# Turning the activations from a second copy in memory instead of on TensorE, in a fused attention and gated-MLP kernel

## The chip, the cores and the metric

The kernel runs on one core of one Trainium2 chip. The metric is the device time of one execution in microseconds. Three runs of the kernel before gave 1763.13 to 1763.9 us, with a median of 1763.62 us. Engines are called as in the profile: PE is TensorE, DVE VectorE, ACT ScalarE, POOL GpSimd, SP the engine whose queue starts most DMAs.

## What is computed

The input x is 2048 rows of 512. Each row is normalised (mean taken away, divided by its standard deviation), and the normalised rows xn go into two branches that are multiplied at the end:

```python
xn = _layernorm(x, axis=-1)
s = _A_ref(xn, A_k_cache, A_v_cache, A_wq, A_wo)      # attention, 32 heads of 128, last 512 keys
g = _silu(_B_ref(xn, B_w_in, B_w_sp, B_b_sp, B_w_out)) # gated MLP
return x + s * g

# in _A_ref
q = (x @ wq).reshape(B, Sq, Hq, Dh)                    # then per head:
scores = einsum("bhqd,bhkd->bhqk", q, k) * Dh ** -0.5
o = einsum("bhqk,bhkd->bhqd", softmax(scores), v);  out = o @ wo
# in _B_ref
z = _gelu(x @ w_in); z1, z2 = z[..., :Fh], _layernorm(z[..., Fh:])
out = (z1 * (einsum("ts,bsf->btf", w_sp, z2) + b_sp[None, :, None])) @ w_out
```

All of it is float32. [...]

## The kernel before

A product `x @ w` needs x with its 512 columns on the partitions. x comes from memory with rows on the partitions, so each tile of 128 rows is normalised and then turned by four TensorE transposes against an identity matrix into one PSUM bank (`flip`, L215). From there ACT casts the high part and DVE or POOL subtracts it from the whole (`rest`, L59), which gives the low part.

The 16 row tiles are two halves of eight. The queries are made by a seven-product scheme over 2 x 2 blocks (`q_products`, L473): besides blocks of x itself it needs four sums of blocks, called T1 to T4, as high and low parts. They are built from tile p and tile 4 + p of a half, p from 0 to 3.

The program is one list written by hand. After a prologue that normalises and turns tiles 0 to 3 (`ln_open`, `ln_apply`, `ln_flip`) comes a loop over steps t from -7 to 529. In each step every engine's queue gets its work in a fixed order: a turn of one early tile, the split of the probabilities of an earlier block (`shares`, t - 11), whatever the tables `todo`, `ends` and `loads` hold for this step, one score tile of 128 x 512 (`score`), products of the next queries, probabilities times values (`pv`, t - 13), the output projection (`outp`, t - 18), and the 32 x 32 transposes of the step before (`turn`). Each engine takes its list in order, and so does SP's DMA queue: a wait holds up all that stands behind it.

Two places of it matter here.

- **The opening's second turn.** In steps -3 to 0 `t_sums(p)` turns tile p once more and `row_sums` (L250 to L252, DVE) makes three sums of its PSUM bank and of the turned tile 4 + p, which stands in `sacc`. In the step after, `t_split(p)` casts four quarters on ACT (L263) and subtracts four times on POOL. Score 0 stands in step 0 behind `t_sums(3)`. A score is read by DVE (`nm`, L500, the row maximum), then by ACT (`prob`, L502, the exponential). Scores, outputs and early pieces of the MLP product take turns on the four PSUM buffers called ps_3 (`ps_step`). In steps -2 to 2 these are, the second turns left away, in order: a piece, a piece, score 0, a piece, score 1, a piece, score 2; score 2 comes into the buffer of score 0. The exponential frees a score's buffer.
- **The second half's x.** `later_x(p)` handles tiles 8 + p and 12 + p, in a list of steps that begins at t = 30 and goes on every 2.6 steps until t = 214. It loads both tiles as rows (pool `xq`, tiles called rawx, five buffers), takes the statistics on DVE (L177), scales the tile on ACT (L315), turns it on TensorE into a ps_a bank (L215), and from that bank makes copies (ACT), low parts and sums (DVE, deferred to the end of the step by the list `late`). All parts go to memory and come back when the second half starts.

POOL's share of a steady step is the low part of the probabilities (`pT_l<-pL,pT_h`, L59), which `pv` needs two steps later (L540), and beside it the low parts of weights (`wl<-raw,wh`, `x<-wq`) and sums of weights (L442). Statistics go through `ln_scale`, which ends in a power on POOL (L75).

Of the kernel before, what the change touches and what calls it, by code (L numbers as in the profile page):

```python
# [17 lines left out]
P = 128  # L18
S, D = 2048, 512
H, DH, W = 32, 128, 512  # L20
NT = S // P
NC = D // P
# [12 lines left out]
T8 = NT // 2  # L35
# [2 lines left out]


@with_exitstack  # L40
def mixer_kernel(ctx: ExitStack, tc: tile.TileContext, x, wh, w_in, w_sp, b_sp, w_out, out):

# [7 lines left out]
    nc = tc.nc  # L50
# [3 lines left out]
    dram = ctx.enter_context(tc.tile_pool(name="dram", bufs=1, space=DRAM))  # L54
# [3 lines left out]
    def rest(engine, lo, whole, hi):  # L58
        engine.tensor_tensor(lo, whole, hi.bitcast(F32), op=OP.subtract)  # L59

    late = []
# [10 lines left out]
    def rsqrt(var, y, n, v, engine=nc.gpsimd):  # L72

        engine.tensor_scalar(v[:, :n], var, EPS, None, op0=OP.add)
        nc.gpsimd.tensor_tensor(y[:, :n], v[:, :n], power[:, :n], op=OP.pow)  # L75

    stats = ctx.enter_context(tc.tile_pool(name="stats", bufs=2))
# [9 lines left out]
    ap = att.enter_context(tc.tile_pool(name="ap", bufs=2))  # L87
# [74 lines left out]
    def halves(t):  # L162
        return t.rearrange("p (c q) -> p c q", q=P)
# [9 lines left out]
    def tile_stats(t, key, k):  # L173
        if k == 0:
            mv[key] = stats.tile([P, 2, 2], F32, name="mv", bufs=5)
        stt = stats.tile([P, 6], F32, name="stt", bufs=4)
        nc.vector.bn_stats(stt, t)  # L177
        nc.vector.bn_aggr(mv[key][:, k, :], stt)
# [4 lines left out]
        ln_scale(len(tiles), key)  # L183

    def ln_scale(n, key):
        r = stats.tile([P, 2], F32, name="rs_r", bufs=5)
        tmp[key] = stats.tile([P, 2], F32, name="rs_t", bufs=4)
        rsqrt(mv[key][:, :n, 1], r, n, tmp[key], nc.vector)
        for k in range(n):
            rx[key + k] = mv[key][:, k, 0:1], r[:, k:k + 1]  # L190

    def ln_open(i):
        a, b = next(g for g in GROUPS if g[0] <= i < g[1])
# [18 lines left out]
    def flip(t, late=False):  # L212
        ps = ps_acc.tile([P, NC, P], F32, name="ps_a") if late else ps_step.tile([P, NC, P], F32, name="ps_3")
        for c in range(NC):
            nc.tensor.transpose(ps[:, c, :], t[:, c * P:(c + 1) * P], ident)  # L215
        return ps
# [31 lines left out]
    def row_sums(ps, y, o):  # L248

        nc.vector.tensor_tensor(o[:, :256], y[:, :256], ps[:, :256], op=OP.subtract)  # L250
        nc.vector.tensor_tensor(o[:, 256:], ps[:, :256], y[:, 256:], op=OP.add)
        nc.vector.tensor_tensor(y[:, :256], ps[:, 256:], o[:, 256:], op=OP.subtract)  # L252

    def t_sums(p):
# [41 lines left out]

    def later_x(p):

        a, b = T8 + p, T8 + 4 + p
        t, nb = {}, {}  # L300
# [6 lines left out]
        def row_stats():  # L307
            ln_scale(2, 100 * (p + 1))
            for k, i in enumerate((a, b)):
                mean, r = rx[100 * (p + 1) + k]  # L310
                nb[i] = tmp[100 * (p + 1)][:, k:k + 1]
                nc.gpsimd.tensor_scalar(nb[i], mean, r, -1.0, op0=OP.mult, op1=OP.mult)

        def apply(i):
            nc.scalar.activation(t[i], t[i], AF.Identity, bias=nb[i], scale=rx[100 * (p + 1) + (i == b)][1])  # L315

        def parts(i, n):
            ps = flip(t[i], True).rearrange("p c q -> p (c q)")
            x = t["x", n] = xq.tile([P, 512], F32, name="rawx")
            nc.scalar.copy(x, ps)  # L320
            if n:
                st = t[0, 1] = xq.tile([P, 512], F32R, name="rawx")
                nc.scalar.copy(st[:, :256], ps[:, :256])
                late.append((rest, nc.vector, st[:, 256:], ps[:, :256], st[:, :256]))
                late.append((rest_f32, t[b][:, 256:], ps[:, 256:], x[:, :256]))
            else:
                late.append((sums, ps, t["x", 1], t[b], t[a]))

        def rest_f32(to, x0, x1):
            nc.vector.tensor_tensor(to, x0, x1, op=OP.subtract)  # L330

        def sums(ps, x, y, o):
            nc.vector.tensor_tensor(o[:, :256], x[:, :256], ps[:, :256], op=OP.subtract)
            nc.vector.tensor_tensor(o[:, 256:], ps[:, :256], y[:, 256:], op=OP.add)
            nc.vector.tensor_tensor(y[:, :256], ps[:, 256:], o[:, 256:], op=OP.subtract)

        def store(*ks):
            for k in ks:
                if k in WHOLE:
                    src, h = {"T1": (a, 0), "T2": (a, 1), "T4": (b, 0), "T3": (b, 1)}.get(k) or (("x", k[1]), k[0])  # L340
                    nc.sync.dma_start(xd[1, k][:, :, p * P:(p + 1) * P], halves(t[src][:, 256 * h:256 * h + 256]))
                else:
                    nc.sync.dma_start(xd[1, k][:, :, :, p * P:(p + 1) * P],
                                      t[k].bitcast(F32).rearrange("p (a c q) -> p a c q", a=2, q=P))

        seq = [load, None, None, lambda: tile_stats(t[a], 100 * (p + 1), 0), lambda: tile_stats(t[b], 100 * (p + 1), 1),
               row_stats, None,
               lambda: apply(b),
               lambda: parts(b, 1),
               lambda: apply(a),  # L350
               None,
               lambda: parts(a, 0)] + [None] * 5
        stores = {10: ((0, 1), (1, 1)), 13: ((0, 0), (1, 0)), 14: ("T2",), 15: ("T1",), 16: ("T3",), 17: ("T4",)}
        return [(f, stores.get(n, ())) for n, f in enumerate(seq + [None])], store


# [209 lines left out]

    T0, T1 = -QL, NSTEP + OL
    NG = NBLK // 4
    todo, mid = {}, {}

    def at(t, f, *args):
        todo.setdefault(t, []).append((f, args))
# [70 lines left out]
    for p in range(4):  # L643
        seq, store = later_x(p)
        for k, (f, ks) in enumerate(seq):
            t = max(t + 2, 30 + 13 * n // 5)
            while k in (8, 11) and t % 4 != 2:
                t += 1
            for key in ks:
                at(t, store, key)  # L650
            if f:
                (mid if k in (8, 11) else todo).setdefault(t, []).append((f, ()))
            n += 1

    load_x(0, 1)
# [72 lines left out]
    for t in range(T0, T1):  # L728
        if t % 4:
            load_all(t)  # L730
        bq, cq = divmod(t + QL, 4)
        bm, cm = divmod(t - ML, 4)
        bp, cp = divmod(t - PL, 4)
        bo, jo = divmod(t - OL, 4)
        i = t + XL
        if i < T8:
            ln_flip(i)
        if 0 <= bm < NBLK:
            shares(bm, cm)
        for f, args in todo.get(t, ()):  # L740
            f(*args)
        if 0 <= t < NSTEP:
            score(t)
        if i + 2 < T8:
            ln_apply(rows[i + 2], i + 2)
        if t in FILL:
            z1_piece(*FILL[t])
        if 0 <= bq < 4:
            qproj(bq, cq)
        g, s = divmod(t + LEAD, 16)  # L750
        if 0 < g < NG:
            q_products(g, s)
        for f, args in mid.get(t, ()):
            f(*args)
# [12 lines left out]
        if t in DRAIN:  # L767
            z1_out(*DRAIN[t], ps)
        if 0 <= t - 1 < NSTEP:
            turn(t - 1)  # L770
        if t % 4 == 2 and 0 <= t // 4 - 1 < NBLK:
            turned(t // 4 - 1)
        while late:
            f, *args = late.pop(0)
            f(*args)
        if t % 4 == 0:
            load_all(t)
        for f, *args in ends.get(t, ()):
            f(*args)
# [425 lines left out]
```

## Time and profile before

| | |
|---|---|
| three runs, median | 1763.62 us |
| profiled execution, its own time | 1763.41 us |
| its span in the profile | 1761.6 us |
| PE busy | 1754.7 us |
| DVE / ACT / POOL busy | 1491.0 / 1186.7 / 1226.6 us |
| granted TensorE clock, mean | 1.0 |
| DMA | 394.25 MB, 224 GB/s |

The span runs from the first to the last instruction that the profile shows; the profiled execution's own time has 1.8 us more, around the span. Busy time adds an engine's instructions up. A row of the timeline has the start in microseconds from the span's start, the duration, the engine, the line of the kernel, the operation and what it writes and reads; `x4` merges four that follow each other; a bracket tells how long the engine sat idle before it and what ended that.

### The profile page before, as it was taken

What the parts mean: (1) busy time and instruction counts of PE and PEld (TensorE: products, weight loads), DVE (VectorE), ACT (ScalarE), POOL (GpSimd) and SP (SyncE); (2) the same over time, 40 slices, a digit from 0 to 9 for tenths busy, and PEclk for the clock granted to TensorE, in tenths of its full rate; (3) what the DMA queues carried; (4) which work ended last, traced back from release to release, by engine and by line L of the source; (5) the groups of instructions that cost most, each with busy time, mean ns of one, the idle gap of its engine ahead of it and who ended that gap; (6) DMA issues with size and microseconds to landing.
All of it is one profiled execution on the core that took longest, in us unless ns stands there. A gap on an engine that the chain in (4) does not pass through costs nothing.

```text
span 1761.6 us, 28515 instructions
## 1 busy us (share of the span) xinstructions
PE 1754.7 (100%) x8463; PEld 1506.7 (86%) x8463; DVE 1491.0 (85%) x2470; ACT 1186.7 (67%) x2621; POOL 1226.6 (70%) x1151
## 2 busy tenths in 40 slices
PE   9999999999999999999999999999999999999999
PEld 8888888888888888888888888888888899999997
DVE  6789989898998989988888888888888647887875
ACT  5777777777777777777777777777777546543333
POOL 2889888888888889878888888888888411000032
PEclk9999999999999999999999999999999999999999
DMA  5688887888888889787887877877788652655496
GB/s 203 209 236 253 247 248 233 248 240 236 251 241 239 250 231 272 217 262 223 224 224 221 229 227 220 226 222 219 232 226 247 216 194 86 224 187 177 148 257 206
DMA packets 171708, 394.25 MB, mean 224 GB/s; under 512 B 23840, under 2 KB 53792, under 8 KB 152352
## 3 DMA queue, kind: packets, MB, share of 16 engines
q1 hardware_dynamic: 166944, 386.80, 74.8%
q10 hardware_dynamic: 4608, 5.64, 0.9%
q8 instruction: 66, 1.08, 0.3%
q14 instruction: 90, 0.74, 0.1%
HBM read 229.55 MB, written 162.79 MB: 223 GB/s over the span
## 4 chain that ended last, share of the span: by engine, by line
PE 98%; DMA 1%; DVE 0%; ACT 0%; issue 0%; SPq 0%; ACTq 0%
PE ps_a L473 17%; PE ps L65 13%; PE ps L67 13%; PE ps L66 13%; PE ps L906 11%; PE ps_a L540 6%; PE ps_a L539 6%; PE ps_a L538 6%; PE ps_a L67 2%; PE ps_a L66 2%; PE ps_a L65 2%; PE ps_f L67 1%; PE ps_f L66 1%; PE ps_f L65 1%; PE ps_f L906 1%; DMA pL<-p_dram 1%
## 5 line engine op out<-in xcount | busy, mean ns | idle before, releaser
L59 POOL TENSOR_TENSOR pT_l<-pL,pT_h 128x512 fp32r<-128x512 f32 x507 | 658.0, 1301 | 185.1 <-ACT pT_h L530 176.1
L502 ACT ACTIVATE prob<-ps,nm 128x512 f32<-128x512 f32 x512 | 354.0, 691 | 339.7 <-DVE nm L500 331.6
L562 DVE SCALAR_TENSOR_TENSOR sacc<-ps,sums,sacc 128x512 f32<-128x512 f32 x496 | 369.8, 746 | 119.2 <-PE ps L67 114.0
L473 PE MATMUL ps_a<-x,x 128*128 128x512 f32 x1266 | 365.3, 389 | 0.0
L511 DVE STREAM_TRANSPOSE pL<-prob 128x512 f32<-128x512 f32 x512 | 358.8, 701 | 0.5 <-ACT prob L502 0.4
L500 DVE TENSOR_REDUCE nm<-ps 128x1 f32<-128x512 f32 x512 | 340.3, 665 | 3.0 <-PE ps L67 2.9
L530 ACT CAST pT_h<-pL 128x512 fp32r<-128x512 f32 x512 | 318.4, 622 | 9.2 <-ACT z L380 4.2
L473 PEld LDWEIGHTS ps_a<-x,x 128*128 128x128 f32 x1266 | 237.7, 188 | 49.2 <-issue 0.2
L59 POOL TENSOR_TENSOR wl<-raw,wh 128x512 fp32r<-128x512 f32 x186 | 241.7, 1299 | 10.9 <-ACT wh L145 10.9
L65 PE MATMUL ps<-wh,qT_h 128*128 128x512 f32 x512 | 199.7, 390 | 0.3 <-DVE sacc L562 0.2
L538 PE MATMUL ps_a<-pT_h,wh 128*128 128x512 f32 x512 | 199.9, 390 | 0.0
L67 PE MATMUL ps<-wh,qT_l 128*128 128x512 f32 x512 | 199.6, 390 | 0.0
L540 PE MATMUL ps_a<-pT_l,wh 128*128 128x512 f32 x512 | 199.4, 389 | 0.0
L65 PE MATMUL ps<-wh,oT_h 128*128 128x512 f32 x512 | 199.3, 389 | 0.0
L66 PE MATMUL ps<-wl,qT_h 128*128 128x512 f32 x512 | 199.3, 389 | 0.0
L539 PE MATMUL ps_a<-pT_h,wl 128*128 128x512 f32 x512 | 199.3, 389 | 0.0
L67 PE MATMUL ps<-wh,oT_l 128*128 128x512 f32 x512 | 199.2, 389 | 0.0
L66 PE MATMUL ps<-wl,oT_h 128*128 128x512 f32 x512 | 199.2, 389 | 0.0
L906 PE MATMUL ps<-b,x 128*128 128x344 f32 x1248 | 191.8, 316 | 0.0
L906 PEld LDWEIGHTS ps<-b,x 128*128 128x128 f32 x1248 | 191.5, 188 | 0.0
L59 POOL TENSOR_TENSOR b<-b 128x512 fp32r<-128x512 f32 x2 | 2.5, 1292 | 189.5 <-DMA x<-s_dram 189.5
L59 POOL TENSOR_TENSOR x<-wq,x 128x256 fp32r<-128x256 f32 x177 | 131.1, 741 | 0.0
(216 smaller groups left out, 3039.5 us busy)
## 6 DMA issues: line engine op xcount, KB each, us to landing
p_dram<-pL SPq DMA_DIRECT2D x128, 1024.0 KB, 4.7
pL<-p_dram SPq DMA_DIRECT2D x256, 192.0 KB, 4.0
raw<-wh SPq DMA_DIRECT2D x188, 256.0 KB, 6.1
pL<-p_dram SPq DMA_DIRECT2D x256, 128.0 KB, 4.0
x<-w_sp SPq DMA_DIRECT2D x24, 1024.0 KB, 5.1
pL<-p_dram SPq DMA_DIRECT2D x256, 64.0 KB, 3.9
wq<-wh SPq DMA_DIRECT2D x60, 256.0 KB, 5.6
z_dram<-z ACTq DMA_DIRECT2D x32, 172.0 KB, 3.3
```

The costliest lines, as they stand in the source:

```text
L59: engine.tensor_tensor(lo, whole, hi.bitcast(F32), op=OP.subtract)
L65: nc.tensor.matmul(ps, lh, rh, start=first, stop=False)
L66: nc.tensor.matmul(ps, lh, rl, start=False, stop=False)
L67: nc.tensor.matmul(ps, ll, rh, start=False, stop=last)
L473: nc.tensor.matmul(qps[g, bank], wt["q", g, k][a][:, c * P:(c + 1) * P], X[g * 2 // H][ORDER[k]][:, b, c], start=first, stop=r == 5, skip_ ...
L500: nc.vector.tensor_reduce(nm, ps, axis=AX.X, op=OP.max, negate=True)
L502: nc.scalar.activation(prob[t], ps, AF.Exp, bias=nm, accum_out=sums[b][:, j:j + 1])
L511: nc.vector.transpose(pL[b][:, :, j * P:j * P + P].rearrange("p a (c q) -> p a c q", q=Q), prob.pop(t).rearrange("p (a c q) -> p a c q", a ...
L530: nc.scalar.copy(h, p)
L538: nc.tensor.matmul(pps[b], vh, ph, start=c == 0, stop=False)
L562: nc.vector.scalar_tensor_tensor(at, ps, rs, at, op0=OP.mult, op1=OP.add)
L906: nc.tensor.matmul(ps, a, b, start=k != "P4" and c == 0 and m == 0, stop=c == RP - 1 and m == 2, skip_group_check=True)
```

## The change

The kernel gets a second copy of x, `xt`, laid out on the host so that tile i's 512 columns are on the partitions already (partition, four column blocks, 128 rows). Twelve of the twenty turns on TensorE go: those of `t_sums(0..3)` and the eight of `later_x`. The turns of the prologue and of steps -7 to -4 stay.

With rows along the free axis a tile can't be scaled by one number per partition. So mean and scale, two numbers per row, which stand one per partition, are stored to memory as rows of 128 (`keep_rows`, 4 bytes from each partition) and read back with every partition getting the same row (`spread`). `normalise` then subtracts the mean row and multiplies by the scale row, over 128 x 512, each as one instruction with two SBUF inputs. In the opening DVE does that in steps -4 to -1, before the three sums, which now read SBUF twice instead of PSUM once. In the second half POOL does it; the high part is cast on ACT, its rest subtracted on POOL, and four sums are made on DVE from SBUF. ACT's scaling and copies out of PSUM, and POOL's `nb` (L312), go away. `rsqrt` writes the scale into the statistics tile instead of a tile of its own.

```diff
-        r = stats.tile([P, 2], F32, name="rs_r", bufs=5)
-        tmp[key] = stats.tile([P, 2], F32, name="rs_t", bufs=4)
-        rsqrt(mv[key][:, :n, 1], r, n, tmp[key], nc.vector)
+        r = mv[key][:, :, 1]
+        tmp[key] = stats.tile([P, 2], F32, name="rs_t", bufs=9)
+        rsqrt(r[:, :n], r, n, tmp[key], nc.vector)
...
+    row_dram = [dram.tile([n, P], F32, name="row_dram") for n in (8, 4, 4, 4, 4)]
+    xturned = {}
+    def keep_rows(d, n, key, k=2):
+        nc.sync.dma_start(d[n:n + 2 * k].rearrange("m p -> p m"), mv[key][:, :k].rearrange("p k m -> p (k m)"))
+    def spread(t, d):
+        nc.sync.dma_start(t, d.rearrange("m p -> (m p)").partition_broadcast(P))
+    def load_turned(i):
+        t = xturned[i] = xq.tile([P, 512], F32, name="rawx")
+        nc.sync.dma_start(t, xt[i].rearrange("p c q -> p (c q)"))
+    def normalise(engine, i, row, op):
+        t = halves(xturned[i])
+        engine.tensor_tensor(t, t, row.unsqueeze(1).broadcast_to([P, NC, P]), op=op)
+    def open_rows():
+        for i in range(4):
+            keep_rows(row_dram[0], 2 * i, i, 1)
+        for i in range(4):
+            load_turned(i)
+    def open_spread():
+        rows0[0] = ap.tile([P, 16, P], F32, name="pL", bufs=4)
+        spread(rows0[0][:, :8].rearrange("p k q -> p (k q)"), row_dram[0])
+    def open_normalise(i):
+        for m, op in ((0, OP.subtract), (1, OP.mult)):
+            normalise(nc.vector, i, rows0[0][:, 2 * i + m], op)
...
-        row_sums(flip(sacc[:, p, :]).rearrange("p c q -> p (c q)"), sacc[:, 4 + p, :], sacc[:, p, :])
+        row_sums(xturned.pop(p), sacc[:, 4 + p, :], sacc[:, p, :])
... in later_x(p):
+        def load_rest():
+            t["row"] = xq.tile([P, 512], F32, name="rawx")
+            spread(t["row"], row_dram[1 + p])
+            for i in (a, b):
+                load_turned(i)
+        def scaled(i, m, op):
+            n = 2 * (i == b) + m
+            normalise(nc.gpsimd, i, t["row"][:, n * P:n * P + P], op)
+        def part():
+            st = t[0, 1] = xq.tile([P, 512], F32R, name="rawx")
+            sl = xturned[b][:, :256]
+            nc.scalar.copy(st[:, :256], sl)
+            rest(nc.gpsimd, st[:, 256:], sl, st[:, :256])
+        def sums(k):
+            b11, b21, b12, b22 = quarters()
...
+            to, x0, x1, op = (("T1", b12, b11, OP.subtract), ("T3", b22, b12, OP.subtract),
+                              ("T2", b11, t["T3"], OP.add), ("T4", b21, t["T2"], OP.subtract))[k]
+            late.append((sum_of, t[to], x0, x1, op))
-               row_stats, None,
-               lambda: apply(b),
-               lambda: parts(b, 1),
-               lambda: apply(a),
+               lambda: ln_scale(2, key),
+               lambda: keep_rows(row_dram[1 + p], 0, key),
+               load_rest,
                None,
-               lambda: parts(a, 0)] + [None] * 5
+               lambda: scaled(b, 0, OP.subtract),
+               lambda: scaled(b, 1, OP.mult),
+               lambda: scaled(a, 0, OP.subtract),
+               lambda: scaled(a, 1, OP.mult),
+               part,
+               lambda: sums(0), ... lambda: sums(3)]
...
     for p in range(4):
+        at(-4 + p, open_normalise, p)
         at(-3 + p, t_sums, p)
         at(-2 + p, t_split, p)
+    ends.setdefault(-7, []).append((open_rows,))
+    ends.setdefault(-6, []).append((open_spread,))
...
+        "xt": a["A_x"][0].reshape(NT, P, NC, P).transpose(0, 3, 2, 1),
```

How this stands in the engines' lists is shown at three places. First DVE in steps -4 to 0, from the last sum of the turn of tile 7 (L244) to the maximum of score 0 (L500). Before, the three sums of a tile read a PSUM bank (ps_538 and so on); rows of p = 1 are left out:

```order
L244 TENSOR_TENSOR sacc<-ps_500,sacc 128x256
L775 SCALAR_TENSOR_TENSOR qT_l<-ps_a,qT_h 128x512
L250 TENSOR_TENSOR sacc<-sacc,ps_538 128x256
L251 TENSOR_TENSOR sacc<-ps_538,sacc 128x256
L252 TENSOR_TENSOR sacc<-ps_538,sacc 128x256
```

The same place of DVE's list now, with the normalising instructions (L269), up to the maximum of score 0:

```order
L244 TENSOR_TENSOR sacc<-ps_513,sacc 128x256
L269 TENSOR_TENSOR rawx<-rawx,pL 128x512 x2
L817 SCALAR_TENSOR_TENSOR qT_l<-ps_a,qT_h 128x512
L250 TENSOR_TENSOR sacc<-sacc,rawx 128x256
L251 TENSOR_TENSOR sacc<-rawx,sacc 128x256
L252 TENSOR_TENSOR sacc<-rawx,sacc 128x256
L269 TENSOR_TENSOR rawx<-rawx,pL 128x512 x2
L250 TENSOR_TENSOR sacc<-sacc,rawx 128x256
L251 TENSOR_TENSOR sacc<-rawx,sacc 128x256
L252 TENSOR_TENSOR sacc<-rawx,sacc 128x256
```

This repeats for the last two tiles before L543 takes score 0's maximum (it was L500): eight instructions of 512 stand in front of it that weren't there, and the twelve sums have two SBUF inputs instead of one.

Second SP's queue in the opening, from the loads of the first weights to the store of a block of x (L305, L272 before), now:

```order
L473 DMA wq<-wh 128x512 x2
L258 DMA row_dram<-mv 128x2x1 x4
L265 DMA rawx<-xt 128x512 x4
L261 DMA pL<-row_dram 128x1024
L106 DMA raw<-wh 128x512
L305 DMA x_dram_109<-x_400 128x2048
```

The nine in the middle (L258, L265, L261) are new; before, the load L106 followed on the two of wq.

Third POOL's list where `later_x(0)` normalises (about step 55): the four instructions over 128 x 512 of L269 stand some low parts of probabilities (pT_l) and of weights apart; wl and x are low parts of weights.

```order
L269 TENSOR_TENSOR rawx<-rawx 128x512
L59 TENSOR_TENSOR pT_l<-pL,pT_h 128x512
L59 TENSOR_TENSOR wl_2346<-raw,wh_2345 128x512
L59 TENSOR_TENSOR x_767<-wq,x_767 128x256
L59 TENSOR_TENSOR pT_l<-pL,pT_h 128x512 x2
L59 TENSOR_TENSOR x_767<-wqs,x_767 128x256
L269 TENSOR_TENSOR rawx<-rawx 128x512
L59 TENSOR_TENSOR pT_l<-pL,pT_h 128x512 x2
L59 TENSOR_TENSOR x_767<-wq,x_767 128x256
L269 TENSOR_TENSOR rawx<-rawx 128x512
```

Before, the same list held only the other rows.

More of the change, by code (lines that the diff above doesn't have):

```diff
@@ L40, in mixer_kernel @@
 @with_exitstack
-def mixer_kernel(ctx: ExitStack, tc: tile.TileContext, x, wh, w_in, w_sp, b_sp, w_out, out):
+def mixer_kernel(ctx: ExitStack, tc: tile.TileContext, x, xt, wh, w_in, w_sp, b_sp, w_out, out):
     nc = tc.nc
@@ L317, in parts @@
[L317 to L327, printed above, removed]
@@ new lines, in scaled, with quarters, sum_of @@
+        def scaled(i, m, op):
+            n = 2 * (i == b) + m
+            normalise(nc.gpsimd, i, t["row"][:, n * P:n * P + P], op)
+        def quarters():
+            return [xturned[i][:, 256 * h:256 * h + 256] for i in (a, b) for h in range(2)]
+        def part():
[3 more added lines that the diff above has]
+            rest(nc.gpsimd, st[:, 256:], sl, st[:, :256])
+        def sum_of(to, x0, x1, op):
+            nc.vector.tensor_tensor(to, x0, x1, op=op)
@@ new lines, in sums @@
+        def sums(k):
+            b11, b21, b12, b22 = quarters()
+            if k == 0:
+                for n in ("T1", "T3"):
+                    t[n] = xq.tile([P, 512], F32, name="rawx")
+                t["T2"], t["T4"] = t["T1"][:, 256:], t["T3"][:, :256]
+                t["T1"], t["T3"] = t["T1"][:, :256], t["T3"][:, 256:]
+            to, x0, x1, op = (("T1", b12, b11, OP.subtract), ("T3", b22, b12, OP.subtract),
+                              ("T2", b11, t["T3"], OP.add), ("T4", b21, t["T2"], OP.subtract))[k]
+            late.append((sum_of, t[to], x0, x1, op))
@@ L339, in store @@
                 if k in WHOLE:
-                    src, h = {"T1": (a, 0), "T2": (a, 1), "T4": (b, 0), "T3": (b, 1)}.get(k) or (("x", k[1]), k[0])
-                    nc.sync.dma_start(xd[1, k][:, :, p * P:(p + 1) * P], halves(t[src][:, 256 * h:256 * h + 256]))
+                    src = t[k] if k in TS else quarters()[2 * k[1] + k[0]]
+                    nc.sync.dma_start(xd[1, k][:, :, p * P:(p + 1) * P], halves(src))
                 else:
@@ L568, in mixer_kernel @@
     NG = NBLK // 4
[L569 removed]
+    todo = {}
     def at(t, f, *args):
@@ L651, in mixer_kernel @@
             if f:
-                (mid if k in (8, 11) else todo).setdefault(t, []).append((f, ()))
+                at(t, f)
             n += 1
@@ L752, in mixer_kernel @@
             q_products(g, s)
-        for f, args in mid.get(t, ()):
-            f(*args)
         if 0 <= bp < NBLK:
```

31 lines of the change are left out of this document (10 added, 21 removed).

## The prediction

> **What bounds the kernel now.** I read the page first (busy times, chain of waits), then who waits on PE, then the timeline at the turns that go away.
>
> ```profile
> PE 1754.7 (100%) x8463; PEld 1506.7 (86%) x8463; DVE 1491.0 (85%) x2470; ACT 1186.7 (67%) x2621; POOL 1226.6 (70%) x1151
> PE 98%; DMA 1%; DVE 0%; ACT 0%; issue 0%; SPq 0%; ACTq 0%
> PE ps L231 <- ACT x L233: 0.5, 1, 0.5
> ```
>
> PE is busy for the whole span and makes up 98% of the chain; its longest wait inside the program, behind the start, is 0.5 us. So an instruction taken off PE shortens the span by the PE time that it took, unless another engine's lateness then stops PE. The question is twofold: what do the twelve turns cost PE, and who becomes late.
>
> **A turn's price on PE.** Starts, not durations, tell it, since matmuls overlap. The list of one step runs from one L538 to the next:
>
> ```profile
> 156.26 0.39 PE L538 MATMUL ps_a<-pT_h,wh 128*128 128x512 f32 x1
> 158.99 0.39 PE L538 MATMUL ps_a<-pT_h,wh 128*128 128x512 f32 x1
> 161.48 0.39 PE L538 MATMUL ps_a<-pT_h,wh 128*128 128x512 f32 x1
> 164.21 0.60 PE L215 MATMUL ps_a<-ident,rawx 128*128 128x128 f32 x4
> 164.56 0.48 PE L538 MATMUL ps_a<-pT_h,wh 128*128 128x512 f32 x1
> 167.41 0.39 PE L538 MATMUL ps_a<-pT_h,wh 128*128 128x512 f32 x1
> 33.25 0.60 PE L215 MATMUL ps<-ident,sacc 128*128 128x128 f32 x4
> 33.60 0.40 PE L65 MATMUL ps_a<-wh,x 128*128 128x344 f32 x1
> 33.84 0.32 PE L66 MATMUL ps_a<-wl,x 128*128 128x344 f32 x1
> 34.00 0.32 PE L67 MATMUL ps_a<-wh,x 128*128 128x344 f32 x1
> ```
>
> A step with three query products takes 2.73 us (156.26 to 158.99). The one with a turn takes 3.08 (161.48 to 164.56) and the next 2.85, 0.35 and 0.12 more: 0.47 us a turn, 3.8 for the second half's eight. In the opening a turn takes 0.35 (33.25 to 33.60), and the matmul behind it 0.24 instead of 0.16: 0.43, and 1.7 for four. Together 5.5 us, if nothing else happens.
>
> [...] DVE gets eight normalising instructions in front of score 0's maximum, and its twelve sums now read SBUF twice. How such instructions fare while POOL works, three neighbours show:
>
> ```profile
> 680.57 1.30 POOL L59 TENSOR_TENSOR wl<-raw,wh 128x512 fp32r<-128x512 f32 x1
> 681.25 1.17 DVE L59 TENSOR_TENSOR x<-x 128x512 fp32r<-128x512 f32 x1
> 681.83 1.74 POOL L59 TENSOR_TENSOR pT_l<-pL,pT_h 128x512 fp32r<-128x512 f32 x1
> ```
>
> DVE's instruction starts 0.62 us before POOL's ends at 681.87, and itself ends 0.55 behind that, at 682.42; POOL's next takes 1.74 instead of 1.30 and ends 1.15 behind DVE's. They went one after the other, not side by side. [...]
>
> ```profile
> 15.16 0.26 POOL L209 TENSOR_SCALAR rs_t<-mv,rs_r 128x1 f32<-128x1 f32 x1
> 11.57 0.61 POOL L209 TENSOR_SCALAR rs_t<-mv,rs_r 128x1 f32<-128x1 f32 x1
> 11.62 1.36 DVE L59 TENSOR_TENSOR wl<-pL,wh 128x344 fp32r<-128x344 f32 x3
> ```
>
> Three DVE instructions follow each other directly from 11.62 to 12.98, one each 0.43 us; POOL's, which takes 0.26 at 15.16, ends at 12.18, behind the first and not behind the third. So I let them alternate: 0.55 for a DVE instruction of 512 columns and half, 0.28, for one of 256; on POOL 1.15 for 512 and, the 0.56 less that 256 columns take alone, 0.6 for 256. Alone DVE needs 0.6 and 0.34 (from 0.43 for 344).
>
> Here is the place, before:
>
> ```profile
> 32.48 0.41 DVE L244 TENSOR_TENSOR sacc<-ps,sacc 128x256 f32<-128x256 f32 x1
> 34.23 0.69 DVE L775 SCALAR_TENSOR_TENSOR qT_l<-ps_a,qT_h 128x512 fp32r<-128x512 f32 x1 [1.33 <-ACT qT_h L400]
> 44.09 0.68 DVE L500 TENSOR_REDUCE nm<-ps 128x1 f32<-128x512 f32 x1
> 44.81 0.69 ACT L502 ACTIVATE prob<-ps,nm 128x512 f32<-128x512 f32 x1 [0.73 <-DVE nm L500]
> 49.32 0.39 PE L65 MATMUL ps<-wh,qT_h 128*128 128x512 f32 x1
> 37.10 2.82 POOL L59 TENSOR_TENSOR x<-sacc,x 128x256 fp32r<-128x256 f32 x4 [6.47 <-ACT x L263]
> 40.86 1.31 POOL L59 TENSOR_TENSOR wl<-raw,wh 128x512 fp32r<-128x512 f32 x1 [0.93 <-ACT wh L145]
> 42.82 2.84 POOL L59 TENSOR_TENSOR x<-sacc,x 128x256 fp32r<-128x256 f32 x4
> 46.30 5.63 POOL L59 TENSOR_TENSOR x<-sacc,x 128x256 fp32r<-128x256 f32 x8
> ```
>
> DVE comes free at 32.9. Two instructions for tile 0, qT_l at its old time, three sums, POOL idle: DVE is through with p = 0 at 36.0. For p = 1 to 3 it has six instructions of 512 and nine of 256, 6 x 0.55 + 9 x 0.28 = 5.8 us. From then on POOL has work nearly without a break: before maximum 0 it fits four low parts of `t_split(0)`, a weight of 512, a sum of weights, four of `t_split(1)`, another sum and three of `t_split(2)`, 13 x 0.6 + 1.15 = 9.0 us. So the maximum starts at 36.0 + 5.8 + 9.0 = 50.8 instead of 44.09, and the exponential ends 1.4 later (44.09 to 45.50 before), at 52.2. Score 2 needs the PSUM buffer of score 0. It started at 49.32 and, four turns fewer ahead of it, would be wanted at 47.6. It waits until 52.2, **2.9 us later than before**. The bounds of this term: if POOL never gets in between, the fifteen take 6 x 0.6 + 9 x 0.34 = 6.7, the exponential ends at 44.1, PE doesn't wait and the opening is 1.7 us shorter; and the lists behind (qT_l of block 1, exponential 1) may add about another microsecond. [...]
>
> **The second half: POOL.** Sixteen instructions of 512 and four of 256 come, eight of L312 go. The window and prices, and the place where PE waits least long for POOL's pT_l:
>
> ```profile
> 111.00:660.00 549.00, 549.00 (x2437) 453.99 (x2436) 494.77 (x841) 411.32 (x953) 479.30 (x451) 1.00 0.85 242
> L59 POOL TENSOR_TENSOR wl<-raw,wh 128x512 fp32r<-128x512 f32 x77 | 99.9, 1297 | 0.0
> L59 POOL TENSOR_TENSOR x<-wq,x 128x256 fp32r<-128x256 f32 x76 | 56.3, 741 | 0.0
> 576.41 1.29 POOL L59 TENSOR_TENSOR pT_l<-pL,pT_h 128x512 fp32r<-128x512 f32 x1
> 579.90 0.39 PE L540 MATMUL ps_a<-pT_l,wh 128*128 128x512 f32 x1
> ```
>
> POOL is idle for 549.0 - 479.3 = 69.7 us, 12.7%; the new work is 16 x 1.3 + 4 x 0.74 = 24, so it fits on the whole. But it comes in bunches: four of 512 and one of 256, 5.9 us, within 13 steps of 2.6 us (156.26 to 161.48 are two), some 34 us with 4.3 idle. POOL falls behind by 1.6, and PE comes 0.9 sooner without two turns: 2.5 against a lead of 2.2 (577.70 to 579.90). I count 0.3 us of waiting a group, **1.3** for four. Its ends are nothing, and 2.5 x 4 = 10 if the lead is used up elsewhere. DVE's four sums a group cost about what its five instructions from PSUM cost. ACT only loses work.
>
> **DMA.** A row store writes 4 bytes from each partition, 256 or 512 pieces. The nearest row has as many pieces, of 512 bytes:
>
> ```profile
> L343 SPq DMA_DIRECT2D x_dram<-rawx x4: 604/1041/1045, 181.7 to 557.5; - x4
> DMA to landing us min/median/max: 3.7/6.4/7.2
> 14.51 0.55 POOL L75 TENSOR_TENSOR rs_r<-rs_t,power 128x1 f32<-128x1 f32 x1 [2.33 <-DVE rs_t L74]
> 32.27 0.33 SPq L272 DMA_DIRECT2D x_dram<-x  x1
> ```
>
> SP issues such a one in 1.04 us, and it lands up to 7.2 us later. The last opening store waits for tile 3's power, which ends at 15.06; landed by 23, read back by about 30. DVE wants it at 32.9, so I cost it at nothing, with 3 us of cover. Behind it on SP stand a weight load and the store of L272, which waited until 32.27 anyway. The extra megabytes (1.5 in the opening, 3 later, of 394) lie beside a DMA share of 0.85.
>
> **Sum**, against the profiled execution's 1763.4: - 3.8 (eight turns) + 1.3 (POOL) + 2.9 (opening, its turns in it) = 1763.8. The median is 0.2 above that execution: **1764.0 us**.
>
> **Rivals.**
> - *DVE keeps its pace* (POOL doesn't get in between, or its low parts come too late to matter): opening - 1.7, so 1763.4 - 1.7 - 3.8 + 1.3 + 0.2 = 1759.4. For it: DVE's instructions for one tile follow each other closely, and PE needs only 47.6. Against: 681.25.
> - *Slower: POOL becomes the bound in the second half.* If its normalising instruction takes as long as the stretched 1.74, each group is 1.8 more behind, 4.3 against 2.2: 2.1 x 4 = 8.4 instead of 1.3. That gives 1764.0 + 7.1 = 1771. It decides from about 1.3 us an instruction on. Against: POOL's same-shaped subtraction has 1297 ns in 77 cases.
> - *Slower: rows late.* [...] In rows: a store landing 7 us later than the slowest above would reach DVE at about 37 instead of 32.9, and score 2 as much later: 1764 + 4 = 1768.
> - *The turns weren't on the path:* the list shows 48 transposes gone, and PE has no idle time to hide them; below 3 in 100.
>
> **How the numbers follow.** My forecast 50%, DVE at its pace 28%, POOL the bound 14%, rows late 5%, others 3%. A measurement here can tell about 0.2%, 3.5 us: faster ends at 1760.1, slower begins at 1767.1. DVE at its pace gives most of faster (24 of 28), with 4 from the forecast's low side: 28%. Slower has 13 + 5 and 6 from the forecast's high side: 24%. Same 48%. The forecast's own range is 1760 to 1768; with both sides 1758 to 1770.
>
> **What would show it.** Right: PE waits some 5 us in all before score 2, with maximum 0 at about 51; L269 on DVE takes over 1 us for p = 1 to 3; in the second half single waits of PE for pT_l, under 1 us each. Wrong: maximum 0 at 43 to 45 (DVE's pace); L269 on POOL far from 1.3 us; PE waiting at more places than these; DVE waiting for row_dram's spread (L261).

## The result and the profile after

The changed kernel takes 1814.01 us (median of 6 runs, 1812.36 to 1816.87) against 1763.76 us before: 1.0287 times the time before, with a 95% interval of 1.0274 to 1.0301. It is 50 us slower; forecast were 1764.0 us and a range of 1758 to 1770. The profiled execution took 1812.94 us, its span 1810.9. From the page of the changed kernel, the busy times and the chain:

```profile
PE 1768.9 (98%) x8415; PEld 1508.5 (83%) x8415; DVE 1525.4 (84%) x2474; ACT 1176.8 (65%) x2605; POOL 1249.9 (69%) x1163
PE 87%; DMA 5%; DVE 4%; POOL 1%; issue 1%; ACT 1%; SPq 0%; ACTq 0%; DVEq 0%; POOLq 0%
```

PE's share of the chain fell from 98% to 87%. The 48 transposes are gone from PE (8463 to 8415 instructions), but its busy time rose: matmuls ran longer, at a lower clock (0.991 of full speed on the mean, before 1.000), as is seen below. Who PE waited for (us in all, times, longest):

```profile
PE ps L65 <- DVE sacc L605: 11.9, 4, 4.5
PE ps_a L65 <- ACT x L233: 6.7, 1, 6.7
PE ps_a L583 <- POOL pT_l L59: 4.9, 9, 0.6
PE ps L67 <- DVE qT_l L59: 4.6, 1, 4.6
PE ps L65 <- ACT prob L545: 4.2, 1, 4.2
```

Before, the longest wait was 0.5 us. Now six are longer than 2 us (three of the four behind L605, and 6.7, 4.6 and 4.2). Where they lie is told by the starts of matching matmuls (one of each score and one of each pT product) in the two traces; how much later one is than its counterpart:

| up to | later than before, us |
|---|---|
| score 0 | 9.6 |
| score 4, end of the opening | 16.3 |
| behind group 1 of the later tiles (240 us) | 24.7 |
| behind group 2 (397 us) | 32.4 |
| behind group 3 (534 us) | 42.2 |
| behind group 4 (669 us) to the end | 49.5 |

Between these places the difference stays nearly as it is, apart from half a microsecond gained at each turn that is gone. So the opening costs 16.3 us, of which 9.6 lie ahead of the place where the prediction looked, and each group costs about 8 us, its saved turns included.

**Ahead of score 0: transfers slow down.** SP's issues, the stretches around them (busy time of each engine, PE's clock, DMA share, GB/s; the last of the three is the kernel before), and what ACT and PE then wait for:

```profile
11.84 3.98 SPq L258 DMA_DIRECT2D row_dram<-mv  x4
15.87 9.43 SPq L265 DMA_DIRECT2D rawx<-xt  x4
```

```profile
10.00:14.00 4.00, 3.85 (x26) 3.55 (x25) 3.57 (x10) 2.51 (x7) 0.81 (x2) 1.00 1.06 398
18.00:22.00 4.00, 4.00 (x29) 3.98 (x28) 3.90 (x10) 1.06 (x3) 0.71 (x1) 1.00 0.74 46
18.00:22.00 4.00, 4.00 (x28) 3.98 (x28) 3.90 (x11) 1.90 (x5) 0.71 (x1) 1.00 0.30 106
```

```profile
DMA to landing us min/median/max: 12.5/12.5/12.5
14.52 0.34 ACTq L424 DMA_DIRECT2D z_dram<-z  x1
25.31 0.45 ACT L423 COPY z<-ps_a 128x344 f32<-128x344 f32 x1 [5.78 <-DMA z_dram<-z]
31.58 0.45 ACT L423 COPY z<-ps 128x344 f32<-128x344 f32 x1 [4.53 <-DMA z_dram<-z]
33.94 0.66 PE L65 MATMUL ps_a<-wh,x 128*128 128x344 f32 x1 [6.74 <-ACT x L233]
```

The four row stores go out from 11.84 us on. The DMA engines move 398 GB/s until 14 us, and 46 GB/s from 18 to 22 us, though they are busy for 0.74 of the time; before, 0.30 of the time was enough for 106 GB/s there. The one row store whose landing the profile shows lands 12.5 us after its issue. The store of z that ACT issued at 14.52 on its own queue is held up too: ACT has two z buffers, so its copy at 25.31 stood for 5.78 us, the one at 31.58 for 4.53, and behind them on ACT stood the casts of x that PE needs: 6.74 us.

**Ahead of score 2: DVE and POOL alternate,** as forecast. From DVE's and POOL's timelines:

```profile
44.07 1.41 DVE L269 TENSOR_TENSOR rawx<-rawx,pL 128x512 f32<-128x512 f32 x2
54.19 0.84 DVE L250 TENSOR_TENSOR sacc<-sacc,rawx 128x256 f32<-128x256 f32 x1
61.62 0.68 DVE L543 TENSOR_REDUCE nm<-ps 128x1 f32<-128x512 f32 x1
54.72 3.84 POOL L59 TENSOR_TENSOR x<-sacc,x 128x256 fp32r<-128x256 f32 x4
63.16 0.79 PE L65 MATMUL ps<-wh,qT_h 128*128 128x512 f32 x1 [4.18 <-ACT prob L545]
```

From the first normalising instruction to the maximum of score 0 it takes 17.55 us (44.07 to 61.62).

**In each group: one DVE sum takes 6 us.** DVE, POOL, PE and the clock around the first sum of the first group:

```profile
227.82 0.70 DVE L554 STREAM_TRANSPOSE pL<-prob 128x512 f32<-128x512 f32 x1
228.44 5.68 DVE L360 TENSOR_TENSOR rawx<-rawx 128x256 f32<-128x256 f32 x1
234.04 0.68 DVE L59 TENSOR_TENSOR qT_l<-ps_a,qT_h 128x512 fp32r<-128x512 f32 x1
242.78 0.39 DVE L360 TENSOR_TENSOR rawx<-rawx 128x256 f32<-128x256 f32 x1
228.06 0.73 POOL L59 TENSOR_TENSOR x<-wq,x 128x256 fp32r<-128x256 f32 x1
233.12 0.71 POOL L59 TENSOR_TENSOR x<-wq,x 128x256 fp32r<-128x256 f32 x1
236.78 1.26 POOL L59 TENSOR_TENSOR pT_l<-pL,pT_h 128x512 fp32r<-128x512 f32 x1 [2.94 <-ACT pT_h L573]
234.78 0.50 PE L67 MATMUL ps<-wh,qT_l 128*128 128x512 f32 x1 [4.65 <-DVE qT_l L59]
236.56 0.63 PE L583 MATMUL ps_a<-pT_l,wh 128*128 128x512 f32 x1
236.00:239.00 3.00, 3.00 (x9) 2.27 (x9) 1.67 (x3) 2.96 (x8) 2.23 (x2) 0.53 0.01 3
```

The next sum, of the same shape, takes 0.39 us at 242.78, when POOL is idle. The one at 228.44 ends at 234.12, that is 0.29 us after POOL's sixth instruction in a row ended (233.12 + 0.71 = 233.83) and POOL had nothing ready. qT_l, the maxima and the output sums stand behind it in DVE's list; PE waits for 4.65 us. Then PE's matmuls of 512 columns follow each other at 0.43 us (235.71, 236.13, 236.56), not at 0.23, for about 3 us: the granted clock is 0.53 there. Behind the long waits of the second and third group it is half for some 6 us (373 to 379 and 516 to 522; the second halves are shown), behind the fourth's 2.70 us it stays at 1.00:

```profile
376.00:379.00 3.00, 3.00 (x8) 2.29 (x8) 1.58 (x3) 2.91 (x8) 2.29 (x3) 0.54 1.00 234
519.00:522.00 3.00, 3.00 (x8) 2.32 (x8) 0.87 (x2) 1.85 (x4) 2.20 (x3) 0.50 0.00 0
```

The four groups have such a sum each: 5.68, 6.33, 6.62 and 5.92 us; their other twelve take 0.4 to 1.5.

### The profile page after: what moved, and what is told of

It reads as the page before. It is cut to its first block, busy times and chain, and to the rows that moved or that the text cites. A ratio compares the mean times of both kernels' runs of the same rounds, so it can differ in the third digit from the quotient of the medians.

```text
span 1810.9 us, 28453 instructions
## 1 busy us (share of the span) xinstructions
PE 1768.9 (98%) x8415; PEld 1508.5 (83%) x8415; DVE 1525.4 (84%) x2474; ACT 1176.8 (65%) x2605; POOL 1249.9 (69%) x1163
## 4 chain that ended last, share of the span: by engine, by line
PE 87%; DMA 5%; DVE 4%; POOL 1%; issue 1%; ACT 1%; SPq 0%; ACTq 0%; DVEq 0%; POOLq 0%
PE ps_a L516 15%; PE ps L65 12%; PE ps L67 12%; PE ps L66 12%; PE ps L948 11%; PE ps_a L583 6%; PE ps_a L581 6%; PE ps_a L582 6%; PE ps_a L67 2%; PE ps_a L65 2%; PE ps_a L66 2%; DMA p_dram<-pL 1%; DMA pL<-p_dram 1%; PE ps_f L67 1%; PE ps_f L65 1%
## 5 line engine op out<-in xcount | busy, mean ns | idle before, releaser
L605 DVE SCALAR_TENSOR_TENSOR sacc<-ps,sums,sacc 128x512 f32<-128x512 f32 x496 | 369.8, 746 | 118.9 <-PE ps L67 113.6
L543 DVE TENSOR_REDUCE nm<-ps 128x1 f32<-128x512 f32 x512 | 340.7, 665 | 2.2 <-PE ps L67 2.2
```

What stands on the lines that cost most here:

```text
L543: nc.vector.tensor_reduce(nm, ps, axis=AX.X, op=OP.max, negate=True)
L605: nc.vector.scalar_tensor_tensor(at, ps, rs, at, op0=OP.mult, op1=OP.add)
```

## The experiments

Theory S: the 4-byte row stores hold up all other transfers. Theory L: DVE's instructions with both inputs in SBUF are kept out by POOL. Rivals: the loads behind the rows on SP's queue, or POOL's work as such. Times are medians beside the kernel before on the same chip (1763.57 to 1763.74).

**The row stores alone.** Added to the kernel before, behind the opening's statistics (open_rows holds the four stores) and in each group; nobody reads them.

```diff
+    ends.setdefault(-7, []).append((open_rows,))
-               row_stats, None,
+               row_stats, lambda: keep_rows(row_dram[1 + p], 0, 100 * (p + 1)),
```

> The kernel before, plus only the row stores of the change at their places (four in the opening, one in each of the four later groups); nobody reads them. Theory S (the 4-byte row stores hold up every other transfer): PE meets a wait of about 7 us before score 0 while the z buffers wait for their landing, as after the change, and each group some 1 to 2 us of waits for pT_l: 9.5 + 4 x 1.5 over 1763.8, about 1779 us. Rival (the stores are harmless; what is late is the read-back and the turned loads behind it on SP's queue): 1764 us.

Measured: 1770.41 us, 1.0040 times before (1.0025 to 1.0055). Issue to landing of the stores (six of the eight landings are in the profile), and PE's waits:

```profile
DMA to landing us min/median/max: 8.9/9.9/13.2
PE ps_a L65 <- ACT x L233: 2.2, 1, 2.2
PE ps L215 <- ACT sacc L210: 1.3, 1, 1.3
```

Against the matching matmuls of before, score 0 comes 6.1 us late, and the four groups add 1.4 in all. So four stores of 1 KB in the opening, which are nobody's input, cost 6 us. The rival (1764 us) falls as the whole cause; but theory S, with its 1779 us, had the stores too large: without the turned loads and the read-back score 0 is 6.1 us late instead of 9.6, and a group without POOL's new work absorbs most of its store.

**Rows in larger pieces.** DVE turns the statistics in blocks of 32 x 32, and a row goes out in four pieces of 128 bytes.

```diff
-        nc.sync.dma_start(d[n:n + 2 * k].rearrange("m p -> p m"), mv[key][:, :k].rearrange("p k m -> p (k m)"))
+        nc.vector.tensor_copy(packs[:, 0, n:n + 2 * k], mv[key][:, :k].rearrange("p k m -> p (k m)"))
+        if key < 3:
+            return
+        nc.vector.transpose(packs[:, 1, :], packs[:, 0, :])
+        for a in range(4):
+            nc.sync.dma_start(d[:, Q * a:Q * a + Q], packs[Q * a:Q * a + n + 2 * k, 1, :])
```

> The changed kernel, its statistics turned by DVE in blocks of 32 x 32 so that a row goes out in four pieces of 128 bytes instead of 128 pieces of 4 bytes; all else as in the change. Theory S: score 0 comes back to about 43 us and the waits for pT_l behind the row stores shrink: 1814 - 9.5 - 4 x 1.5 = 1798 us. The wait ahead of score 2 and one wait of 2.7 to 4.7 us in each group remain. Rival (the length of the round trip matters, not the size of its pieces): 1812 to 1816 us.

Measured: 1803.03 us (1.0221, 1.0206 to 1.0236). PE's waits:

```profile
PE ps L65 <- DVE sacc L613: 11.4, 4, 4.4
PE ps L65 <- ACT prob L553: 6.5, 1, 6.5
PE ps L67 <- DVE qT_l L59: 4.2, 1, 4.2
PE ps L956 <- ACT b L870: 4.1, 1, 4.1
```

The wait for ACT's x and all nine for pT_l are gone, and score 0 comes 1.2 us earlier than before the change. In the opening this edit moves the stores too, from 11.84 to 25.99 us, behind the first burst of loads, so score 0 alone doesn't tell the size of the pieces from their time. The first group does: there the store stands between the same two weight loads of SP's list (issued at 168.56 in the change, at 160.06 here), and some 6 to 10 us behind its issue the two kernels move 14 and 229 GB/s:

```profile
175.00:179.00 4.00, 4.00 (x19) 3.31 (x18) 3.53 (x7) 2.27 (x6) 4.00 (x5) 1.00 0.30 14
166.00:170.00 4.00, 4.00 (x19) 3.30 (x19) 3.53 (x7) 2.23 (x6) 4.00 (x5) 1.00 1.02 229
```

So theory S holds. What stays are the waits for DVE, and one wait is new, in the last stage (L956). Up to the last score the kernel is 26.6 us late instead of 49.5, at the end 37.8: that stage loses another 11.2.

**The sums on POOL.**

```diff
-            late.append((sum_of, t[to], x0, x1, op))
+            nc.gpsimd.tensor_tensor(t[to], x0, x1, op=op)
```

> The changed kernel with the sixteen sums of the second half on POOL instead of DVE, in the same steps. Theory L (a DVE sum with both inputs in SBUF is kept out for as long as POOL's instructions follow each other closely): the four long waits of PE (4.65, 4.45, 4.55, 2.70 us) and the slow clock behind them go, about 6 us a group: 1814 - 24 = 1790 us. Rival (POOL itself is the bound in a group): POOL gets 16 x 0.74 = 12 us more, PE waits longer for pT_l, and the time stays at 1814 us or rises to 1825 us.

Measured: 1786.45 us (1.0129, 1.0114 to 1.0145). PE's waits:

```profile
PE ps_a L65 <- ACT x L233: 5.9, 1, 5.9
PE ps L65 <- ACT prob L545: 4.2, 1, 4.2
PE ps_a L583 <- POOL pT_l L59: 2.6, 6, 0.6
```

With 12 us more on POOL the long waits for DVE are gone (1.6 us for oT_l remain), and those for POOL shrink from 4.9 to 2.6 us. The groups cost 6.0 us in all instead of 33. POOL was never the bound; that rival falls.

**Both, twice.** The first of these two runs puts the packed rows in a new tile, the second in an old one.

> Both edits together: rows stored in pieces of 128 bytes, the second half's sums on POOL. If the two causes are separate their gains add: 1814 - 15.5 - 24 = 1774.5 us, still above the kernel before by the opening's wait ahead of score 2 (about 5 us with the clock), and by POOL's lateness. If both are one cause (a late row makes POOL late, which starves DVE), one edit alone brings most of it, and this gives 1785 to 1795 us.

> The same two edits as in e_packed_sums_pool, with the packed rows in a tile that the kernel already had for padding, so that no tile of the last stage moves. In e_packed_sums_pool PE waited 4.08 us for a GELU at 1500 us and lost 11 us in the last stage, which neither the change nor the other two experiments show. If that came from the place of the new tile, this gives 1781 - 11 = 1770 us; if it belongs to the edits, 1781 us.

Measured: 1780.94 (1.0097, 1.0080 to 1.0114) and 1780.56 us (1.0100, 1.0086 to 1.0114). The tile's place isn't the cause of the loss in the last stage. PE's waits of the second run, the first product of its last stage, and PE's instructions in 50 us of that stage, of this kernel and then of the one with the sums on POOL only:

```profile
PE ps L65 <- ACT prob L553: 6.9, 1, 6.9
PE ps L956 <- ACT b L870: 4.1, 1, 4.1
1498.49 3.76 PE L956 MATMUL ps<-b,x 128*128 128x344 f32 x15 [4.09 <-ACT b L870]
1550.00:1600.00 50.00, 50.00 (x319) 50.00 (x319) 43.46 (x55) 24.18 (x29) 0.00 (x0) 1.00 0.51 170
```

```profile
1550.00:1600.00 50.00, 50.00 (x328) 50.00 (x327) 43.95 (x53) 24.45 (x30) 0.00 (x0) 1.00 0.52 174
```

Up to the last score the second run is 5.1 us late; its end is 16.6 late. Of the 49.5 us there, the packed rows alone take away 22.9, the sums on POOL alone 28.6, and both 44.4: most of what each edit wins is its own, and some 7 us are won by either. The built program says why PE waits at 1498: the last GELU reads PSUM bank 0, which the first product of the last stage writes. That is so in this kernel and in the one with packed rows; in the kernel before, in the change, with the sums on POOL and with the second half alone, none of which has this wait, the GELU reads bank 3. The pools hand out their buffers in an order that the edits shift. Behind the wait PE does 319 instead of 328 instructions in 50 us at full granted clock, to the end of the stage. Why it stays 3% slower isn't known. This loss of 11.2 to 11.5 us stands in all five kernels that have both the new opening and packed rows, and is taken off where their first part is compared.

**The second half alone, with both edits; the opening as before.**

> The same two edits, with the opening as in the kernel before: only the second half's turns go. In e_packed_sums_pool PE ran 8.5 us late behind the opening and 6.5 us late after the four groups, so the groups gain 2.1 us there: 1763.7 - 2.1 = 1761.6 us. Rival (POOL, with 12 us more of sums, keeps PE waiting as soon as PE is not held up by the opening): 1764 to 1768 us.

Measured: 1760.81 us (11 runs, 1760.55 to 1761.24), 0.9984 times before (0.9975 to 0.9993). PE's waits inside the program, and the chain:

```profile
PE ps_a L591 <- POOL pT_l L59: 0.3, 1, 0.3
PE ps L65 <- DVE sacc L613: 0.2, 1, 0.2
PE 96%; DMA 2%; POOL 1%; DVE 1%; issue 0%; ACT 0%; SPq 0%; POOLq 0%; ACTq 0%
```

This version beats both kernels, by 2.9 us over the one before. From the opening on it is up to 3.6 us ahead at the last group and 2.6 at the end.

**The opening without POOL's low parts.** On top of the second run of both edits; ACT copies the values instead.

```diff
-            rest(nc.gpsimd, lo, halves(src), hi)
+            nc.scalar.copy(lo, halves(src))
```

> As e2_packed_sums_pool, but the sixteen low parts of the opening's four sums blocks are not computed: ACT copies the values instead of POOL subtracting. So POOL has next to nothing to do while DVE normalises and sums. Theory L in the opening (DVE and POOL take turns): from 36.4 us on DVE takes 0.69 and 0.42 us an instruction, the maximum of score 0 starts at 47 to 48 instead of 54.2 us, PE waits 1 to 2 instead of 8 us ahead of score 2: 1770 - 7 = 1763 us. Rival (DVE has simply too many instructions there): 1770 us.

This kernel leaves out the low parts of the opening's sums. Measured: 1775.44 us (1.0067, 1.0054 to 1.0081), with the last stage's 11.3 off 1764.1. DVE's timeline in this kernel, to be set beside L250 at 54.19 above:

```profile
34.82 1.42 DVE L277 TENSOR_TENSOR rawx<-rawx,pL 128x512 f32<-128x512 f32 x2 [2.45 <-DMA pL<-row_dram]
41.91 0.43 DVE L250 TENSOR_TENSOR sacc<-sacc,rawx 128x256 f32<-128x256 f32 x1
47.69 0.68 DVE L551 TENSOR_REDUCE nm<-ps 128x1 f32<-128x512 f32 x1
```

With little left on POOL the same list takes 12.9 us instead of 17.8 (34.95 to 52.75 in the kernel that it is built on), and PE waits 3.0 instead of 6.9 us. At the end of the opening it is 2.0 us late instead of 7.4. So most of what remains of the opening's cost once the stores are packed is the alternation with POOL.

**Rows earlier.** Also on top of both edits: the rows go out right behind tile 3's scale, and the normalising instructions move two to three steps forward.

> As e2_packed_sums_pool, with the opening's rows stored as soon as tile 3's scale is there (some 15 us instead of 25 us) and the eight normalising instructions on DVE two to three steps earlier, in its idle time ahead of POOL's low parts. Theory: rows and exclusion together cost the opening's 8.5 us; normalising undisturbed takes 8 x 0.69 = 5.5 us ahead of 36 us, only the twelve sums still alternate with POOL (12 x 0.5 = 6 us more than alone), and score 2 waits about 2 us: 1770 - 6 = 1764 us. If the early rows hold up the z stores as the 4-byte pieces did, score 0 moves back by some microseconds and the time stays at 1768 to 1772 us.

Measured: 1772.72 us (1769.26 to 1775.57; 1.0050, 1.0036 to 1.0064), with the last stage off about 1761. The 6.9 us wait ahead of score 2 is gone; in its place score 0 comes 2.1 us late, behind short waits for DVE's and ACT's x. The packed stores go out at 17.12 us here and the DMA engines still move 171 GB/s from 18 to 22 us and 279 from 22 to 26, so the early place alone doesn't bring the change's 46; but with the turned loads behind them ACT's copy of 27.39 us still waits 3.00 us for a z store. The opening then is 2.4 us late instead of 7.4. It doesn't beat the opening with turns.

**Each part alone.**

> The second half as in the change, the opening as in the kernel before. Between matching steps of the two traces the opening of the change loses 16.3 us and its four groups some 33 us. If the two parts are independent: 1814 - 16.3 = 1797.7 us, with one DVE sum of 5 to 7 us in each group. Rival (the groups suffer because the opening left PE, POOL and the queues late): under 1790 us.

> The opening as in the change, the second half as in the kernel before. If the parts are independent: 1763.7 + 16.3 = 1780 us, with PE waiting about 7 us before score 0 and 4 us before score 2. Rival (what the opening loses is caught up later, since PE has no wait behind it in the kernel before): 1764 to 1770 us.

Measured: 1791.10 us (1785.92 to 1793.14; 1.0152, 1.0135 to 1.0169) and 1779.64 us (1.0091, 1.0074 to 1.0107). The second half alone costs 27.5 us, the opening alone 16.1; together 43.6, the change 50.3. The opening came as expected, the second half 6.6 us below its 1797.7. So most of each part's loss is its own and isn't caught up; of the 6.6 us that the change loses beyond the sum, 3.3 are PE's waits for pT_l and oT_l (5.9 us in the change, 2.6 in the second half alone); the rest wasn't taken apart, and the runs of the second half alone lie 7 us apart themselves.

**Which sum is kept out.** In the first run T3 comes first instead of T1; in the second each sum stands ahead of its step's maximum.

```diff
-            to, x0, x1, op = (("T1", b12, b11, OP.subtract), ("T3", b22, b12, OP.subtract),
+            to, x0, x1, op = (("T3", b22, b12, OP.subtract), ("T1", b12, b11, OP.subtract),
... and the stores of T1 and T3 change places
```

```diff
-            late.append((sum_of, t[to], x0, x1, op))
+            sum_of(t[to], x0, x1, op)
```

> The changed kernel with T3 as the first of each group's sums and T1 as the second (before: T1 first). In the changed kernel it is always the first that takes 5.7 to 6.6 us. If the place decides (the first sum meets POOL at its busiest), T3 takes 5 to 7 us in its stead and the time stays at 1814 us, within 3. If the operation decides (T1 subtracts two different tiles, T3 two halves of one), T3 takes under 1.6 us, and the long one, if POOL is still busy without a break, is T1 one place later; otherwise 1790 to 1800 us.

> The changed kernel with each sum of the second half ahead of its step's maximum on DVE instead of at the step's end behind the turn of the probabilities; nothing else moves. If POOL keeps DVE out as long as its own instructions follow each other closely, wherever the sum stands, four sums again take 4 to 7 us: 1814 us, within 4, and PE's waits move to the maximum. If it is the DVE instruction in front (a turn, directly behind which the sum starts) that decides, all sums take under 1.6 us: about 1792 us.

Measured: 1809.05 us (1803.88 to 1809.14; 1.0251, 1.0236 to 1.0267) and 1812.02 us (1.0275, 1.0259 to 1.0290). From DVE's timeline with T3 first:

```profile
226.51 5.92 DVE L360 TENSOR_TENSOR rawx<-rawx 128x256 f32<-128x256 f32 x1
```

The first sum of a group takes 5.7 to 6.6 us in the change and 5.9 to 6.6 with T3 first, and 4.4 to 6.6 us in the other place: neither the operation nor the instruction in front matters. What does is told by all 14 traces (before, after and the twelve experiments). In them 322 DVE instructions with both inputs in SBUF came while POOL was at work and its next instruction followed within 0.1 us. Twenty were kept out for five to seven of POOL's instructions: in each trace with DVE's sums from SBUF in the second half, the first sum of each group. Each of them came when POOL had worked for 18.3 us or longer without a break (17 or more instructions), and each ended 0.28 or 0.29 us behind a POOL instruction after which POOL had nothing ready for 2.3 us or more. The other 302 got in behind the first POOL instruction, and POOL's run so far was 14.6 us at most. Whether the length of the run decides, or how much work stands ready behind POOL, wasn't told apart. That it takes two inputs in SBUF is seen in the change itself: 41 DVE instructions with one of two inputs in PSUM came in such runs of POOL, and none took over 0.76 us for 512 columns. One of them, when POOL had been at work for 35 us:

```profile
223.51 0.69 DVE L59 TENSOR_TENSOR oT_l<-ps_a,oT_h 128x512 fp32r<-128x512 f32 x1 [0.30 <-ACT oT_h L591]
```

## Why the prediction was wrong

Its sum was 1763.4 - 3.8 + 1.3 + 2.9. Step by step:

- **The turns' price on PE** holds. The second half, freed from both causes, gains 2.6 us; the prediction's own terms for it were 3.8 less 1.3. (That POOL has the sums besides in that kernel is not in those terms.)
- **The opening's alternation** holds, and its size: 17.9 us were forecast from DVE's start to the maximum of score 0 (32.9 to 50.8), 17.55 measured. That score 2 then waits is right too: 4.6 us were forecast (47.6 to 52.2), 4.18 measured. The start was wrong, by 11 us. In part the match is luck: where POOL doesn't disturb it, a tile takes DVE 2.58 us (37.89 to 40.47 in the run without the low parts) instead of the 2.2 that the prediction took, so by this estimate DVE's own pace was put 1 us too low and POOL's turns 1 us too high.
- **"I cost it at nothing" of the row stores is the first step that failed.** The forecast took the row of a store with as many pieces of 512 bytes: landing within 7.2 us. These took 12.5 us (8.9 to 13.2 with the stores alone), and the 3 us of cover that the prediction kept was for DVE only. The harm was done to everybody else: ACT's z stores, on another queue, landed 8.2 us after their issue (median of the four from 10 to 30 us; 1.8 us of eight before), ACT's two z buffers filled, PE stood. (The cover was short as well: with packed rows DVE still waits 2.45 us for them, at 34.82.) Cost 6.1 us alone, and score 0 is 9.6 late with the turned loads and the read-back. With the stores alone the packets under 512 bytes rise from 23840 to 27040, by 3200, and the eight stores have 3072 elements: about a packet for each. Rows that come late had been a rival at 5 in 100, the author's estimate; it looked only at when the rows come back, not at what else was to be moved then.
- **"DVE's four sums a group cost about what its five instructions from PSUM cost" is the second, and the larger: some 22 to 27 us of the 50, the slow clock behind the waits included** (26.6 late instead of 5.1 up to the last score with packed rows, 33 instead of 6 us in the groups without). Before, each sum had one input in PSUM, and 41 DVE instructions of that kind came in POOL's long runs in the change without one that took over 0.76 us; now both are in SBUF. The prediction had shown the exclusion in the opening and sized it at half a microsecond an instruction, and did not carry it to the sixteen sums of the second half. And its model of the exclusion, turn by turn, doesn't hold there: 5.7 to 6.6 us for an instruction of 0.4.
- **POOL's own term** (1.3 us of waits for pT_l) was too small, though its kind was right: POOL's instruction takes what was said, and the waits came singly and under 1 us, but are 4.9 us in all (2.2 with the second half alone):

```profile
L269 POOL TENSOR_TENSOR rawx<-rawx x16: 1283/1292/1314, 196.2 to 639.1; 128x512 f32<-128x512 f32 x16
```

  The rival with POOL as the bound (from 1.3 us an instruction on) is refuted by the sums on POOL.
- **Left out altogether: what a wait costs beyond itself.** Behind the waits of more than 4 us PE's clock is about half for 3 to 6 us. The time lost by it, estimated from the granted clock, is 1.7 us in the opening (0.57 from 34 to 38 us), 1.4 in the first group (3 x 0.47) and some 3 each in the second and third (6 us at about 0.5); between score 2 (13.8 late) and score 4 (16.3) it is 2.4 us by their starts. Together that is some 11 of the 50 us.

The forecast's list of what would show it wrong named "PE waiting at more places than these", which is what happened. The chance of slower (24%) counted small excesses over a bound; no case had one instruction stop two engines for several microseconds.

## What to carry to other kernels

When an operand moves from PSUM to SBUF, the instruction changes its neighbours as well as its length (here four sums took 5.7 to 6.6 us, the other twelve of that shape 0.4 to 1.5): look up for each such DVE instruction, at each place, what POOL does then and for how long it has done so, and give the work to POOL itself if POOL is busy there (1786.45 instead of 1814.01 us here). A transfer is costed by its pieces and by what else is to be moved then, not by its bytes or its own consumer: here four stores of 1 KB in pieces of 4 bytes made score 0 6.1 us late. Turn a column into rows on the chip before it is stored (229 GB/s instead of 14 behind the first group's store). A wait of PE is to be counted with the slow clock behind it, here up to 3 us for a wait of 4.5.

## What the runs showed of the hardware that was not expected

- Behind 1024 pieces of 4 bytes the DMA engines moved 46 GB/s at a busy share of 0.74 (before: 106 at 0.30), and a store on another queue was held up too; in the first group it was 14 GB/s behind 512 such pieces and 229 with pieces of 128 bytes.
- POOL, when it had worked 18.3 us or more without a break, kept a DVE instruction with two SBUF inputs out until it had nothing ready (20 of 20 cases, five to seven instructions, 4.4 to 6.6 us); after runs of up to 14.6 us the two took turns (302 cases).
- Behind PE's wait of 4.65 us the granted clock was 0.53 from 236 to 239 us. It was low behind the other four of the change's five waits of 4.18 us and more too (0.57 from 34 to 38 us, 0.50 from 62 to 66, from 373 to 376 and from 516 to 519); behind the one of 2.70 us it stayed at 1.00. Behind the 2.2 us of the stores alone it was 0.61 from 30 to 34 us, so the length of one wait doesn't tell it by itself.
- Behind one wait of 4.1 us the products of the last stage stayed 3% slower to its end (319 instead of 328 instructions in 50 us) at a granted clock of 1.00. The cause is open.
